# Attention with soft cap and a max-out layer: another order of weight loads, casts and filler matmuls at the start

## The chip, the cores and the metric

The kernel runs on one core of a Trainium2 chip. The metric is the device time of one execution in microseconds (us), as the median over several runs. The engines of the core are named PE (TensorE: matmuls and transposes), ACT (ScalarE: tanh, exp), DVE (VectorE), POOL (GpSimd) and SP (SyncE, which only issues transfers here). Transfers are issued by SP (a hardware queue) and by POOL (a software queue, which also converts float32 to bfloat16 on the way); both use the same 16 DMA engines.

## The reference

Attention over 8 batches and 12 heads, 448 positions, head dimension 64, and then a max-out layer on the 3584 tokens of 768 features:

```python
scores = scale * np.matmul(q, k.transpose(0, 1, 3, 2))
scores = cap * np.tanh(scores / cap)
attn = np.exp(scores - np.max(scores, axis=-1, keepdims=True))
attn = attn / (np.sum(attn, axis=-1, keepdims=True) + 1e-09)
x = np.matmul(attn, v)            # then (8, 12, 448, 64) -> (3584, 768)
g = np.maximum(x @ w1, x @ w2)    # w1, w2: 768 x 1024
out = g @ w_out                   # w_out: 1024 x 768
```

The inputs and the output are float32.

## The kernel before

**The algebra.** max(x w1, x w2) = x w2 + relu(x (w1 - w2)). So the kernel builds `wd_sb` = w1 - w2 and `wm_sb` = w2 w_out once, and computes out = x wm + relu(x wd) w_out. `wm_sb` costs PE work before the first output: `turn_w2(c)` transposes one of six chunks of w2 (8 matmuls against an identity, evicted by DVE into `w2T`), and `premultiply(c, half)` multiplies it with one half of w_out's columns (8 matmuls, evicted into `wm_sb`). Together that is 48 transposes and 96 matmuls.

**Tiles of the attention.** Two heads make a pair, 48 pairs in all; three pairs make a group g (16 groups), and two pairs a step t (24 steps, 0 to 23). `load` brings k, q or v of a group (or of one pair of it) through SP's queue, `cast` turns it to bfloat16 in `kqf` (k and q) or `vp` and `vl` (v). k and q must then be transposed into `qkT`: for pairs 0 to 5 (groups 0 and 1) PE does it with `transposes(i)`, 27 small matmuls and a DVE eviction; from group 2 on one DMA transpose by SP does a group, `cross(g)`. Then `scores(t, p)` makes the scores of one pair (p = 0, 1; three PSUM tiles j = 0, 1, 2) or the remaining keys of both (p = 2), each followed by a tanh on ACT; `ex(t, p)` takes the exponential of a whole p; `total(t)` sums it on PE and turns the sums into reciprocals on DVE (`st`, `rs`, `inv`); `values(t)` multiplies with v; `normalize(t)` writes `xT` on DVE. Step t uses pairs 2t and 2t + 1.

**Filler.** PE work that no step of the attention asks for stands in a list of generators, `fill_q`: first the w2 work, then `moe(b)` for each batch. `F(n)` takes n matmuls from it. Calls of `F` stand by hand between the calls of the attention, and each engine executes its instructions in the order in which they were written; so the numbers in `F` decide how much filler PE does ahead of the next scores. `moe(b)` has 8 groups of 6 matmuls (evicted by a relu on DVE) and for each tile of 128 rows two groups of 14 (evicted by a DVE copy to `osb`).

**Buffers that matter.** `mm_psum` has two tiles, shared by transposes, w2 work and MoE. `s_psum` has two and `v_psum` one; a score tile is free when its tanh is done. w2 itself lies in the tiles that later hold `gT` (the relu's output), so the relus wait until w2 has been used. w1 arrives in the tiles of later outputs (`osb`, and `xT` of batches 2 and 3), and `subtract` on POOL or DVE makes `wd_sb` of it.

**The order at the start.** On POOL's queue, transfers of w2 and w_out (`load_w2`, `load_wo`) alternate with casts: chunk 0, two pieces of w_out, chunk 1, the cast of pair 3, chunk 2, a piece of w_out, a one-element transfer (L517), the last piece of w_out, chunk 3, the casts of pair 4 and of half of v of group 0, chunk 4, the cast of pair 5, chunk 5. A cast waits for its load, and all that follows on POOL waits with it. The one-element transfer writes into the tile that pair 4's k is loaded into, so that SP's load of it (and all behind it on SP's queue) waits for that point of the software queue. Then come the calls of the attention for t = 0 to 3, with `F` between them, from L525 on, and a loop for t = 3 to 23 with 47 matmuls of filler in each pass.

Of the kernel before, what the change touches and what calls it, by code (L numbers as in the profile page):

```python
# [10 lines left out]
def kernel(  # L11
# [105 lines left out]
    def load(g, what, n0=0, n1=L):  # L117
        b, p = divmod(g * L, NP)
        h0, h1 = 2 * (p + n0), 2 * (p + n1)
        src = {"k": k, "q": q, "v": v}[what]  # L120
        t, m, l = raw_of(g, what)
        if g < NT:
            nc.sync.dma_start(
                out=t[:, n0 * S : n1 * S].rearrange("p (n c) -> p n c", c=S),
                in_=rows(src, b, h0, h1).rearrange("(n p) c -> p n c", p=P),
            )
            return
        nc.sync.dma_start(
            out=m[:, 2 * n0 : 2 * n1, :],
            in_=src[b, h0:h1, 0 : NJ * P, :].rearrange("h (p j) d -> p h (j d)", j=NJ),  # L130
        )
        if what == "q":
            nc.sync.dma_start(
                out=l[half(b), 2 * n0 : 2 * n1, :],
                in_=src[b, h0:h1, NJ * P : S, :].rearrange("h p d -> p h d"),
            )
        else:
            for par in range(2):
                nc.sync.dma_start(
                    out=l[64 * par : 64 * par + 64, n0:n1, :],  # L140
                    in_=src[b, h0 + par : h1 : 2, NJ * P : S, :].rearrange("h p d -> p h d"),
                )
# [65 lines left out]
    def load_wo(f, half):  # L208
        hs = slice(half * (DM // 2), (half + 1) * (DM // 2))
        nc.gpsimd.dma_start(  # L210
            out=wo_sb[:, f : f + FH, hs], in_=moe_w_out[f * P : (f + FH) * P, hs].rearrange("(c p) n -> p c n", p=P)
        )
# [5 lines left out]
    def load_w2(c):  # L218
        for part in range(2):
            nc.gpsimd.dma_start(out=w2b[part][:, c, :], in_=x_rows(moe_w2, c)[:, part * DH : (part + 1) * DH])  # L220
# [13 lines left out]
    w2T = {}  # L234

    def turn_w2(c):
        ps = mm_psum.tile([P, 512], f32, name="mm").bitcast(bf16)
        for f in range(FC):
            nc.tensor.transpose(ps[:, f * P : (f + 1) * P], w2b[f // FH][:, c, f % FH * P : (f % FH + 1) * P], ident)
            yield  # L240
        w2T[c] = stage.tile([P, FC * P], bf16, name="w2T", bufs=3)
        nc.vector.tensor_copy(w2T[c], ps)  # L242

    def premultiply(c, half):

        hs = slice(half * (DM // 2), (half + 1) * (DM // 2))
        ps = mm_psum.tile([P, 512], f32, name="mm")
        for f in range(FC):
            nc.tensor.matmul(  # L249
                ps[:, : DM // 2], w2T[c][:, f * P : (f + 1) * P], wo_sb[:, f, hs],  # L250
                start=(f == 0), stop=(f == FC - 1),
            )
            yield
        nc.vector.tensor_copy(wm_sb[:, c, hs], ps[:, : DM // 2])


# [139 lines left out]
    gT = {}  # L396

    def moe(b):
        if b % 2 == 0:
            gT[b // 2] = {}  # L400
        g, x = gT[b // 2], xT[b // 2]
        cs = slice((b % 2) * S, (b % 2 + 1) * S)
        for f in range(FC):
            ps = mm_psum.tile([P, 512], f32, name="mm")
            for c in range(KC):
                nc.tensor.matmul(  # L406
                    ps[:, :S], wd_sb[:, c, f * P : (f + 1) * P], x[:, c, cs], start=(c == 0), stop=(c == KC - 1)
                )
                yield
            if f // FH not in g:  # L410
                g[f // FH] = g_tile(f // FH)
            nc.vector.tensor_relu(g[f // FH][:, f % FH, cs], ps[:, :S])  # L412
        for t in range(3) if b % 2 == 0 else range(3, 7):
            osb = opool.tile([P, DF], f32, name="osb")[:, :DM]
            ts = slice(t * P, (t + 1) * P)
            for half in range(2):
                hs = slice(half * (DM // 2), (half + 1) * (DM // 2))
                ps = mm_psum.tile([P, 512], f32, name="mm")
                for c in range(KC):
                    nc.tensor.matmul(ps[:, : DM // 2], x[:, c, ts], wm_sb[:, c, hs], start=(c == 0), stop=False)  # L420
                    yield
                for f in range(FC):
                    nc.tensor.matmul(  # L423
                        ps[:, : DM // 2], g[f // FH][:, f % FH, ts], wo_sb[:, f, hs], start=False, stop=(f == FC - 1)
                    )
                    yield
                nc.vector.tensor_copy(osb[:, hs], ps[:, : DM // 2])  # L427
                if b == B - 1 and t == 6:
                    o = out[b * S : b * S + NJ * P, hs].rearrange("(p j) n -> p j n", j=NJ)
                    nc.sync.dma_start(out=o[:, NJ - 1, :], in_=osb[:, hs])  # L430
            if b == B - 1 and t == 6:
                continue
            wide = b * NP >= NT * L
            if t == 3:
                for n in range(2):
                    o = out[(b - 1 + n) * S : (b + n) * S, :]
                    to = o[NJ * P : S, :] if (b - 1 + n) * NP >= NT * L else o.rearrange("(r j) n -> r j n", j=R7)[:, R7 - 1, :]
                    nc.sync.dma_start(out=to, in_=osb[64 * n : 64 * n + 64, :])
            else:
                j = t if t < 3 else t - 4  # L440
                o = out[b * S : (b + 1) * S, :]
                if wide:
                    nc.sync.dma_start(out=o[: NJ * P, :].rearrange("(p j) n -> p j n", j=NJ)[:, j, :], in_=osb)
                else:
                    o = o.rearrange("(r j) n -> r j n", j=R7)
                    for n in range(2):
                        nc.sync.dma_start(out=o[:, 2 * j + n, :], in_=osb[64 * n : 64 * n + 64, :])

    fill_q = []
    rate = [1.0, 0.0]  # L450

    def F(n):
        rate[1] += n * rate[0]
        while rate[1] >= 1 and fill_q:
            try:
                next(fill_q[0])
                rate[1] -= 1
            except StopIteration:
                fill_q.pop(0)
        if not fill_q:  # L460
            rate[1] = 0.0
# [21 lines left out]
        for f, a in todo[i]:  # L483
            f(*a)

    def load_and_cast(g, n):
        for what in ("k", "q"):
            load(g, what, n, n + 1)
        for what in ("k", "q"):
            cast(nc.gpsimd, g, what, n, n + 1)  # L490

    for c in range(3):
        fill_q.append(turn_w2(c))
        fill_q.append(premultiply(c, 0))
    for c in range(3, KC):
        fill_q.append(premultiply(c - 3, 1))
        fill_q.append(turn_w2(c))
        if c > 3:
            fill_q.append(premultiply(c - 1, 0))
    fill_q.append(premultiply(KC - 3, 1))  # L500
    fill_q.append(premultiply(KC - 1, 0))
    for c in range(KC - 2, KC):
        fill_q.append(premultiply(c, 1))

    fill_const(nc.vector, 0)
    fill_const(nc.gpsimd, 1)
# [3 lines left out]
    load_w2(0)  # L510
    for f in range(0, FC, FH):
        load_wo(f, 0)
    load_w2(1)
    load_and_cast(1, 0)
    load_w2(2)
    load_wo(0, 1)
    nc.gpsimd.dma_start(out=raw_of(1, "k")[0][:1, S : S + 1], in_=moe_w_out[:1, :1])  # L517
    load_wo(FH, 1)
    load_w2(3)
    load_and_cast(1, 1)  # L520
    load(0, "v")
    cast(nc.gpsimd, 0, "v", halves=(1,))
    load_w2(4)
    load_and_cast(1, 2)
    load_w2(5)  # L525
    for n0, n1 in ((0, 1), (1, L)):
        for what in ("k", "q"):
            cast(nc.vector, 0, what, n0, n1)
# [2 lines left out]
    scores(0, 0, v_psum)  # L531
    ex(0, 0)
    transposes(1)
    F(8)
    scores(0, 1, v_psum)
    ex(0, 1)
    transposes(2)
    load(2, "k")
    load(2, "q")
    load(1, "v")  # L540
    cast(nc.gpsimd, 2, "k")
    cast(nc.gpsimd, 2, "q")
    cast(nc.gpsimd, 1, "v", halves=(1,))
    transposes(3)
    F(8)
    scores(0, 2)
    ex(0, 2)
    F(16)
    scores(1, 0, v_psum)
    ex(1, 0)  # L550
    F(16)
    scores(1, 1, v_psum)
    ex(1, 1)
    cast(nc.vector, 0, "v", halves=(0,))
    F(20)
    transposes(4)
    F(6)
    scores(1, 2)
    ex(1, 2)
    cross(2)  # L560
    for c in range(KC):
        load_w1(c, 0)
    load(3, "k")
    load(3, "q")
    for c in range(3):
        load_w1(c, 1)
    total(0)
    normalize(0, values(0))
    scores(2, 0, js=(0, 1))
    transposes(5)  # L570
    scores(2, 0, js=(2,))
    ex(2, 0)
    F(14)
    scores(2, 1, v_psum)
    F(6)
    cast(nc.vector, 1, "v", halves=(0,))
    F(8)
    scores(2, 2)
    ex(2, 1)
    total(1)  # L580
    normalize(1, values(1))
    F(4)

    scores(3, 0, v_psum)
    ex(2, 2)
# [6 lines left out]
        subtract(c, 1, nc.gpsimd)  # L592
    scores(3, 1, js=(0, 1))
    cross(3)
    for c in range(3, KC):
        load_w1(c, 1)
    load(2, "v")
    cast(nc.gpsimd, 2, "v")
    load(3, "v")
# [94 lines left out]
```

## Time and profile before

| | before |
|---|---|
| median of 13 runs | 354.59 us (352.87 to 356.83) |
| the profiled execution | 355.27 us |
| its span on the core | 353.3 us |
| PE busy | 329.1 us (93%) |
| ACT busy | 277.4 us (78%) |
| DVE busy | 229.8 us (65%) |
| POOL busy | 107.6 us (30%) |
| DMA, moved | 61.78 MB, mean 175 GB/s |

The span runs from the first to the last instruction of the core; all times inside the profile count from its start. Busy is the time in which an engine executes something; the difference to the span is idle time. A line of the page's slices has one digit for each of 40 equal slices of 8.8 us: the busy share in tenths. In a wait, the engine and line named first waited for what stands behind the arrow: total, how often, longest. In the chain of waits, each line is a start, a duration and what ran or was transferred.

### The profile page before, as it was taken

To read this page: it belongs to the slowest core of one execution; us is meant where nothing else is said; L and a number is where in the kernel's file an instruction comes from. 1 tells how busy PE (TensorE), PEld (TensorE's weight loads), DVE (VectorE), ACT (ScalarE), POOL (GpSimd) and SP (SyncE) were. 2 spreads that over 40 slices of the span, in tenths; PEclk is the share of its full clock that TensorE was granted. 3 is DMA by queue.
4 is the path that set the end of the run, shared out by engine and by line. 5 is a ranking of instruction groups with operands and counts; after the bars stand their busy time and mean duration, and the time that the engine had idled before them with its cause. 6 is when DMAs were issued, how large, how long until landed. Compare 5 with 4: busy or idle time off the path is not lost.

```text
span 353.3 us, 6833 instructions
## 1 busy us (share of the span) xinstructions
PE 329.1 (93%) x2722; PEld 164.9 (47%) x2722; DVE 229.8 (65%) x413; ACT 277.4 (78%) x241; POOL 107.6 (30%) x184
## 2 busy tenths in 40 slices
PE   3686797999999999999999999999999999999995
PEld 1343343445544554444544454445535554555563
DVE  5325387657768676877678667876777767883421
ACT  3948399989998999989998999999979998800000
POOL 6618367160341244124314431342144130000000
PEclk9999699999999999999999999999999999999999
DMA  7999897999798649973995599629973931012022
GB/s 220 195 263 270 160 300 167 258 248 225 119 254 253 126 130 232 312 158 102 236 297 111 136 234 315 145 78 215 303 171 94 198 105 45 2 46 89 0 91 89
DMA packets 106047, 61.78 MB, mean 175 GB/s; under 512 B 62624, under 2 KB 101024, under 8 KB 106016
## 3 DMA queue, kind: packets, MB, share of 16 engines
q1 hardware_dynamic: 102144, 58.21, 64.9%
q0 software_dynamic: 3872, 3.15, 5.9%
q8 instruction: 21, 0.34, 0.4%
q14 instruction: 10, 0.08, 0.1%
HBM read 42.47 MB, written 11.01 MB: 151 GB/s over the span
## 4 chain that ended last, share of the span: by engine, by line
PE 77%; DMA 8%; ACT 7%; DVE 4%; issue 1%; POOL 1%; SPq 1%; DVEq 0%; POOLq 0%
PE mm L423 21%; PE mm L406 19%; PE mm L420 16%; PE v L373 6%; PE s L310 5%; ACT tanh L311 4%; ACT expo L316 3%; PE s L307 2%; DMA gT<-in_moe_w_dram 2%; PE v L379 2%; PE v L310 2%; DMA qr<-in_q_dram 2%; DMA kr<-in_moe_w_out_dram 2%; DMA vr<-in_v_dram 2%; PE s L357 2%; DVE xT L394 1%
## 5 line engine op out<-in xcount | busy, mean ns | idle before, releaser
L316 ACT ACTIVATE expo<-tanh 128x2688 bf16<-128x2688 bf16 (+1 forms) x72 | 140.3, 1950 | 0.2
L311 ACT ACTIVATE tanh<-s 128x896 bf16<-128x896 f32 x122 | 106.5, 915 | 30.1 <-PE s L310 19.9
L423 PE MATMUL mm<-wo_sb,gT 128*128 128x384 bf16 x448 | 85.8, 327 | 0.0
L406 PE MATMUL mm<-xT,wd_sb 128*128 128x448 bf16 x384 | 78.7, 353 | 2.4 <-DVE gT L412 1.8
L420 PE MATMUL mm<-wm_sb,xT 128*128 128x384 bf16 x336 | 66.2, 327 | 0.0
L423 PEld LDWEIGHTS <-gT 128*128 128x128 bf16 x448 | 42.4, 98 | 34.4 <-issue 8.2
L427 DVE COPY osb<-mm 128x384 f32<-128x384 f32 x56 | 31.1, 556 | 41.4 <-PE mm L423 41.0
L406 PEld LDWEIGHTS <-wd_sb 128*128 128x128 bf16 x384 | 35.8, 98 | 40.5 <-issue 10.0
L412 DVE TENSOR_SCALAR gT<-mm 128x448 bf16<-128x448 f32 x64 | 39.4, 622 | 18.9 <-PE mm L406 18.4
L654 POOL COPY mark<-inv 1x1 f32<-1x1 f32 x18 | 3.2, 177 | 140.7 <-DVE inv L363 125.4
L420 PEld LDWEIGHTS <-xT 128*128 128x128 bf16 x336 | 31.6, 98 | 26.2 <-issue 6.3
L311 ACT ACTIVATE tanh<-v 128x896 bf16<-128x896 f32 x46 | 42.5, 925 | 0.0
L373 PE MATMUL v<-expo,vp 128*32 128x448 bf16 x576 | 36.8, 362 | 0.0
L359 DVE STREAM_TRANSPOSE st<-s 128x448 f32<-128x448 f32 x24 | 15.6, 650 | 27.3 <-PE s L357 17.4
L394 DVE TENSOR_TENSOR xT<-v,inv 128x448 bf16<-128x448 f32 x48 | 27.8, 620 | 4.0 <-PE v L379 1.7
L310 PE MATMUL s<-qkT 64*128 64x448 bf16 x196 | 28.2, 364 | 0.9 <-DVE qkT L281 0.8
L338 DVE TENSOR_TENSOR esum<-esum,expo 128x896 bf16<-128x896 bf16 x40 | 25.4, 634 | 1.0
L336 DVE TENSOR_TENSOR esum<-expo 128x896 bf16<-128x896 bf16 x40 | 25.6, 640 | 0.0
L334 DVE TENSOR_TENSOR esum<-esum,expo 64x896 bf16<-64x896 bf16 x40 | 24.6, 616 | 1.3
L310 PEld LDWEIGHTS <-qkT 64*128 64x128 bf16 x288 | 10.6, 95 | 24.4 <-issue 18.6
L249 PE MATMUL mm<-wo_sb,w2T 128*128 128x384 bf16 x96 | 19.2, 343 | 2.9 <-DVE w2T L242 2.9
L373 PEld LDWEIGHTS <-vp 128*32 128x32 bf16 x576 | 15.7, 99 | 11.0 <-issue 1.5
(66 smaller groups left out, 263.1 us busy)
## 6 DMA issues: line engine op xcount, KB each, us to landing
kr<-in_k_dram SPq DMA_DIRECT2D x14, 576.0 KB, 6.9
qr<-in_q_dram SPq DMA_DIRECT2D x14, 576.0 KB, 7.6
vr<-in_v_dram SPq DMA_DIRECT2D x14, 576.0 KB, 5.0
out_dram<-osb SPq DMA_DIRECT2D x20, 384.0 KB, 6.0
out_dram<-osb SPq DMA_DIRECT2D x16, 192.0 KB, 2.7
osb<-in_moe_w_dram SPq DMA_DIRECT2D x8, 256.0 KB, 4.5
gT<-in_moe_w_dram POOLq DMA_DIRECT2D x12, 128.0 KB, 7.2
wo_sb<-in_moe_w_out_dram POOLq DMA_DIRECT2D x4, 384.0 KB, 8.5
```

The costliest lines, as they stand in the source:

```text
L310: nc.tensor.matmul(s[:, m, :S], k0[r, j * P : (j + 1) * P], qTn[r, :])
L311: nc.scalar.activation(tanh[t, p][:, 2 * j : 2 * j + 2, :], s[:, :, :S], AF.Tanh, scale=scale / cap)
L316: nc.scalar.activation(expo[t, p], tanh[t, p][:, 0:n, :], AF.Exp, scale=float(cap))
L336: nc.vector.tensor_add(d, e_of(t, ab, 0), e_of(t, ab, 1))
L338: nc.vector.tensor_add(d, d, e_of(t, ab, 2))
L373: nc.tensor.matmul(ps[r, :S], vp[g % 2][:, 2 * n + h, j, u::2], e_of(t, ab, j)[:, h, :], start=(j == 0), stop=False,)
L394: nc.vector.tensor_mul(x_of(t, u), ps[:, u, :S], inv[t])
L406: nc.tensor.matmul(ps[:, :S], wd_sb[:, c, f * P : (f + 1) * P], x[:, c, cs], start=(c == 0), stop=(c == KC - 1))
L412: nc.vector.tensor_relu(g[f // FH][:, f % FH, cs], ps[:, :S])
L420: nc.tensor.matmul(ps[:, : DM // 2], x[:, c, ts], wm_sb[:, c, hs], start=(c == 0), stop=False)
L423: nc.tensor.matmul(ps[:, : DM // 2], g[f // FH][:, f % FH, ts], wo_sb[:, f, hs], start=False, stop=(f == FC - 1))
L427: nc.vector.tensor_copy(osb[:, hs], ps[:, : DM // 2])
```

## The change

On POOL's queue all of w2 and w_out is issued in one row, and the casts follow; the one-element transfer stands behind chunk 2. The cast of pair 3 moves to DVE. Transposes and scores of pairs 0 to 3 stand ahead of any w2 work. The w2 work has another order, in which a chunk is transposed one product ahead of its use, and the numbers in `F` follow it. `total(0)` and `normalize(0)` stand later than `values(0)`, and so on for step 1. On SP's queue two halves of w1 stand ahead of `cross(2)`, and all six second halves ahead of `cross(3)`. Last, the generators (`turn_w2` below, `premultiply` and `moe` in the same way) yield ahead of each matmul and not behind it, and `F` runs a generator to its end with its last matmul, so that a group's eviction is issued with its last matmul and not with the next call of `F`.

```diff
 def turn_w2(c):
-        ps = mm_psum.tile([P, 512], f32, name="mm").bitcast(bf16)
         for f in range(FC):
+            yield
+            if f == 0:
+                ps = mm_psum.tile([P, 512], f32, name="mm").bitcast(bf16)
             nc.tensor.transpose(ps[:, f * P : (f + 1) * P], w2b[f // FH][:, c, f % FH * P : (f % FH + 1) * P], ident)
-            yield
...
     def F(n):
         rate[1] += n * rate[0]
         while rate[1] >= 1 and fill_q:
+            g = fill_q[0]
+            if g is not rate[2]:
+                rate[2] = g
+                next(g)
+            rate[1] -= 1
             try:
-                next(fill_q[0])
-                rate[1] -= 1
+                next(g)
             except StopIteration:
                 fill_q.pop(0)
...
-    def load_and_cast(g, n):
+    def load_and_cast(g, n, eng=nc.gpsimd):
...
-    for c in range(3):
-        fill_q.append(turn_w2(c))
-        fill_q.append(premultiply(c, 0))
-    for c in range(3, KC):
-        fill_q.append(premultiply(c - 3, 1))
-        fill_q.append(turn_w2(c))
-        if c > 3:
-            fill_q.append(premultiply(c - 1, 0))
...
+    w2wo((0, T), (1, T), (0, 0), (2, T), (1, 0), (2, 0), (0, 1), (1, 1), (3, T), (2, 1), (3, 0), (4, T), (3, 1))
+    w2wo((4, 0), (5, T), (4, 1), (5, 0), (5, 1))
...
-    load_w2(1)
-    load_and_cast(1, 0)
-    load_w2(2)
-    load_wo(0, 1)
+    for c in range(1, 3):
+        load_w2(c)
     nc.gpsimd.dma_start(out=raw_of(1, "k")[0][:1, S : S + 1], in_=moe_w_out[:1, :1])
-    load_wo(FH, 1)
-    load_w2(3)
-    load_and_cast(1, 1)
-    load(0, "v")
-    cast(nc.gpsimd, 0, "v", halves=(1,))
-    load_w2(4)
-    load_and_cast(1, 2)
-    load_w2(5)
+    for f in range(0, FC, FH):
+        load_wo(f, 1)
+    for c in range(3, KC):
+        load_w2(c)
...
     transposes(1)
-    F(8)
     scores(0, 1, v_psum)
     ex(0, 1)
+    load_and_cast(1, 0, nc.vector)
     transposes(2)
+    transposes(3)
+    load_and_cast(1, 1)
+    load(0, "v")
+    cast(nc.gpsimd, 0, "v", halves=(1,))
+    load_and_cast(1, 2)
...
-    transposes(3)
-    F(8)
     scores(0, 2)
     ex(0, 2)
-    F(16)
+    F(28)
     scores(1, 0, v_psum)
     ex(1, 0)
-    F(16)
+    F(28)
     scores(1, 1, v_psum)
     ex(1, 1)
+    F(24)
+    transposes(4)
     cast(nc.vector, 0, "v", halves=(0,))
-    F(20)
-    transposes(4)
-    F(6)
     scores(1, 2)
     ex(1, 2)
+    for c in range(2):
+        load_w1(c, 0)
     cross(2)
-    for c in range(KC):
+    for c in range(2, KC):
         load_w1(c, 0)
     load(3, "k")
     load(3, "q")
-    for c in range(3):
+    for c in range(KC):
         load_w1(c, 1)
-    total(0)
-    normalize(0, values(0))
+    F(16)
     scores(2, 0, js=(0, 1))
-    transposes(5)
+    x0 = values(0)
     scores(2, 0, js=(2,))
     ex(2, 0)
-    F(14)
-    scores(2, 1, v_psum)
-    F(6)
+    transposes(5)
+    total(0)
+    F(8)
+    scores(2, 1, js=(0, 1))
+    normalize(0, x0)
+    F(4)
+    scores(2, 1, js=(2,))
     cast(nc.vector, 1, "v", halves=(0,))
-    F(8)
+    F(4)
     scores(2, 2)
     ex(2, 1)
+    F(8)
     total(1)
     normalize(1, values(1))
-    F(4)
+    F(2)
...
     cross(3)
-    for c in range(3, KC):
-        load_w1(c, 1)
```

More of the change, by code (lines that the diff above doesn't have):

```diff
@@ L246, in premultiply @@
         hs = slice(half * (DM // 2), (half + 1) * (DM // 2))
-        ps = mm_psum.tile([P, 512], f32, name="mm")
         for f in range(FC):
+            yield
+            if f == 0:
+                ps = mm_psum.tile([P, 512], f32, name="mm")
             nc.tensor.matmul(
@@ L252, in premultiply @@
             )
-            yield
         nc.vector.tensor_copy(wm_sb[:, c, hs], ps[:, : DM // 2])
@@ L398, in moe @@
     def moe(b):
-        if b % 2 == 0:
-            gT[b // 2] = {}
-        g, x = gT[b // 2], xT[b // 2]
+        g, x = gT.setdefault(b // 2, {}), xT[b // 2]
         cs = slice((b % 2) * S, (b % 2 + 1) * S)
         for f in range(FC):
-            ps = mm_psum.tile([P, 512], f32, name="mm")
             for c in range(KC):
+                yield
+                if c == 0:
+                    ps = mm_psum.tile([P, 512], f32, name="mm")
                 nc.tensor.matmul(
@@ L408, in moe @@
                 )
-                yield
             if f // FH not in g:
@@ L417, in moe @@
                 hs = slice(half * (DM // 2), (half + 1) * (DM // 2))
-                ps = mm_psum.tile([P, 512], f32, name="mm")
                 for c in range(KC):
+                    yield
+                    if c == 0:
+                        ps = mm_psum.tile([P, 512], f32, name="mm")
                     nc.tensor.matmul(ps[:, : DM // 2], x[:, c, ts], wm_sb[:, c, hs], start=(c == 0), stop=False)
+                for f in range(FC):
                     yield
-                for f in range(FC):
                     nc.tensor.matmul(
@@ L425, in moe @@
                     )
-                    yield
                 nc.vector.tensor_copy(osb[:, hs], ps[:, : DM // 2])
@@ L449 @@
     fill_q = []
-    rate = [1.0, 0.0]
+    rate = [1.0, 0.0, None]
     def F(n):
@@ L489, in load_and_cast, with w2wo @@
         for what in ("k", "q"):
-            cast(nc.gpsimd, g, what, n, n + 1)
-    for c in range(3):
-        fill_q.append(turn_w2(c))
-        fill_q.append(premultiply(c, 0))
-    for c in range(3, KC):
-        fill_q.append(premultiply(c - 3, 1))
-        fill_q.append(turn_w2(c))
-        if c > 3:
-            fill_q.append(premultiply(c - 1, 0))
[L500 to L503, printed above, removed]
+            cast(eng, g, what, n, n + 1)
+    def w2wo(*parts):
+        for c, half in parts:
+            fill_q.append(turn_w2(c) if half is None else premultiply(c, half))
+    T = None
+    w2wo((0, T), (1, T), (0, 0), (2, T), (1, 0), (2, 0), (0, 1), (1, 1), (3, T), (2, 1), (3, 0), (4, T), (3, 1))
+    w2wo((4, 0), (5, T), (4, 1), (5, 0), (5, 1))
     fill_const(nc.vector, 0)
```

## The prediction

> **What bounds the kernel now.** I read the page first: the totals, then the 40 slices.
>
> ```profile
> span 353.3 us, 6833 instructions
> PE 329.1 (93%) x2722; PEld 164.9 (47%) x2722; DVE 229.8 (65%) x413; ACT 277.4 (78%) x241; POOL 107.6 (30%) x184
> PE   3686797999999999999999999999999999999995
> ACT  3948399989998999989998999999979998800000
> ```
>
> From slice 8 on PE has no gap, so from about 66 us PE sets the pace; ACT is close behind (38.35 of 40 us in 110 to 150). What can be won lies in the first seven slices of 8.8 us. So I asked for stretches of 5 us (columns: stretch, then PE, PEld, DVE, ACT, POOL busy, PE clock, DMA share, GB/s).
>
> ```profile
> 25.00:30.00 5.00, 3.99 (x31) 1.97 (x29) 3.11 (x6) 4.97 (x5) 2.57 (x6) 1.00 1.08 307
> 30.00:35.00 5.00, 2.49 (x43) 1.51 (x40) 2.12 (x4) 4.23 (x4) 4.71 (x11) 1.00 1.13 247
> 35.00:40.00 5.00, 2.93 (x28) 1.12 (x32) 0.12 (x1) 1.72 (x2) 3.27 (x5) 0.61 0.63 113
> 40.00:45.00 5.00, 4.87 (x73) 2.31 (x66) 3.23 (x6) 1.95 (x4) 0.00 (x0) 0.71 1.06 244
> ```
>
> PE idles 7.9 us between 15 and 45, and from 36.1 to 42.9 it runs at half clock (0.50 in stretches of 1 us from 37 to 42): the 5.5 us of matmuls there would take half as long warm, 2.7 us less. Another 2.6 us idle lie in 45 to 60. These 13 us are all there is to take. The chain of waits, then the waits, say what the hole is:
>
> ```profile
> 20.76 6.75 DMA vr<-in_v_dram
> ...
> 29.40 7.63 DMA gT<-in_moe_w_dram
> ...
> 37.07 0.39 PE mm L239 x2
> 37.47 0.75 PE s L307 x2
> ```
>
> ```profile
> PE mm L239 <- DMA gT<-in_moe_w_dram: 4.5, 1, 4.5
> ACT tanh L311 <- PE s L307: 4.0, 1, 4.0
> ACT tanh L311 <- PE s L310: 3.0, 1, 3.0
> ```
>
> GpSimd stood behind v of group 0 until 27.5, cast it, and only at 29.40 issued w2 chunk 4. It landed at 37.0. PE stopped at its transpose with scores(1, 2) behind it; ACT dried up for 4.0 and then 3.0 us.
>
> **What the skill says.** "TensorE: Matmul & The Clock Gate", HAM clock gate: the array starts, and after an idle window of about 3.4 us falls back, at half clock, and about 3.4 us of work bring it back. The trace agrees: nothing between 32.6 and 37.07, half clock until 42.9; premultiplies take 0.34 us apart until 20, 0.18 from 22.5. "DMA: Bandwidth & Descriptors", Queues, rings and completion order: an engine takes turns between its queues packet by packet. The trace does not show that. By its packet records GpSimd's queue moved nothing until 7.0 (first issue 3.06), alone moved 192 to 207 KB per us from 10 to 21, and nothing from 23 to 33; at both borders one queue fades out while the other fades in. That looks like the order of issue, and I use it. The same page puts the fixed cost of a GpSimd transfer at about 2 us; here it hides behind a backlog.
>
> **The change, part by part.** *Transfers.* Bytes and count stay the same. GpSimd now issues all twelve w2 halves and four w_out pieces before any cast. At 200 KB/us a w2 chunk (256 KB as written) takes 1.3 us and a w_out piece (384 KB) 1.9. The one-element marker that holds back SP's pair 4 stands behind one w_out piece less: it lands at 19.9 - 1.9 = 18.0. GpSimd's later issues wait for landings eight transfers back, the last for the marker, so it is done at about 18.7 and no cast is held, since k of pair 4 lands later. In order of issue the second w_out half lands at 21.7, w2 chunks 3, 4, 5 at 23, 24.3, 26.7. SP's loads follow: k, q of pair 4 at 25 and 26, v at 28.8, group 2's q at 36.5 (35.0 before), v of group 1 at 38. Casting that q takes 1.14 + 0.51: cross(2) goes out at 38.3 (37.91 before).
>
> *Walk of PE and ACT*, with durations of the trace (tanh 0.92, large exp 2.44, small 0.96, evictions 0.56 to 0.69, a group of eight premultiplies 1.47 warm and 2.74 cold, eight w2 transposes 1.1 cold and 0.6 warm, values 2.26, total 1.1). VectorE casts pair 3 at 10.6 to 11.9 (GpSimd did it at 9.0 to 11.1; k and q landed at 9.0 and 10.5), so transposes 2 and 3 run 12.0 to 14.3 and scores(0, 2) at 14.3; its tanh waits only for exp(0, 1), to 17.0 instead of 20.95. The first 28 matmuls of w2 work fill 15.0 to 20.1: 1.2, a wait of 0.1 for chunk 1 (16.2), 1.1, 2.5, 0.3. Tanh(1, 0) starts at 20.5 (24.36 before). The next 28 (0.3 + 0.7 eviction overlapped, three groups of 1.47) end at 25.9, tanh(1, 1) at 26.3 (29.28). Then 24 (1.5, 0.6, 1.5), transposes 4 (0.85) and scores(1, 2), tanh 31.7 (38.25). Sixteen more, and scores(2, 0) at 34.0, tanh 34.4 (43.20). VectorE's half of the v cast (1.29 + 0.43 from 32.0) hides behind those 16; values(0) runs 34.6 to 36.9, transposes 5 to 38.1, total(0) to 39.2, a group to 40.7, tanh(2, 1) at 41.1 (48.12). Exp(2, 1) ends at 47.05, after scores(2, 2) at 43.0. VectorE then is the late one: v of group 1 cast from 42.6 to about 44.5 (1.93 + 1.14 beside GpSimd before), two evictions, total(1)'s statistics to 47.4; scores(3, 0) at 47.7, tanh 48.1 (53.80): 5.7 ahead. PE has no hole of 3.4 us, so it stays warm. cross(2) lands by 44.5.
>
> *From there ACT paces* (14.7 us busy of 15.6 between tanh(3, 0) and tanh(4, 1)); scores(4, 1), at 67.91 before, would stand at 62.2. But now all six second halves of w1 stand ahead of cross(3) on SP's queue, three more than before (0.79 MB, 2.6 us). From cross(2): four w1 halves to 47, group 3 to 52.5, six w1 halves to 57.5, cross(3) 4 us more: it lands at 62.5 (64.5 before). A stall of 0.3: the advance is 5.4.
>
> *Filler.* Up to scores(4, 1) the calls of F add to 166 now, 150 before: 16 more MoE matmuls of 0.194 us are behind us, 3.1. moe(0) has 132 matmuls; 6 + 47 + 47 + 38 = 138 are asked of it before moe(1) is appended at the end of t = 5, so six calls find nothing and their cover for the softmax adds is gone: at most 6 x 0.194 = 1.2 back, taken as 1.0.
>
> *Evictions with the last matmul.* The same instructions, earlier on VectorE's queue. What it can win is the PE waits for evictions after 66 us, 1.8 + 0.4 by the waits; what it can lose is a statistic of total queued behind an eviction of 0.56. VectorE is 74% busy there and the eviction follows a matmul that PE is just doing; I take 0, between -2 and +4.
>
> *Other moves at nothing:* two w1 halves ahead of cross(2) (1.6 us of transfers, behind v of group 1, which cross(2) waits behind anyway; without the 3 us between its landing and scores(3, 0) they would cost that), total(0) after values(0) (normalize is not asked for before scores(2, 1)).
>
> Sum: -5.4 - 3.1 + 1.0 = -7.5. The profiled execution took 355.27, of which 353.3 is the span; its span becomes 345.8. The median of the runs is 354.59, 0.7 below that execution, and it becomes 347.1; I say 347.0.
>
> **Rivals.** *cross(3) decides.* If packets are slower behind w1 (197 KB/us was seen at 31 us, with small pieces) and it lands at 66, the advance is 1.9 and the sum -1.9 - 3.1 + 1.0 = -4.0: 350.6. For it: DMA share above 1 from 45 to 55. Against: 2 us idle at 56 to 58 before.
>
> *Data come no sooner.* DMA is saturated from 4 to 36 in both and cross(2) is no earlier; if scores(3, 0) stays at 52.85, only the filler is won, 3.1 - 1.0: 352.5. Against: before, cross(2) landed at 43.5, nine us ahead of its use.
>
> *SP's queue goes first.* Then the second w_out half waits from 19.3 until SP's 4.2 MB are through, 36.5; PE, stopped at 25 for 11.5 us, also goes cold (1.7), and scores(2, 0) comes at 47.2 instead of 42.7, less 22 matmuls of filler (3.6): about 355.5. Against: 117 KB of GpSimd's queue still moved between 21 and 22 while SP's had begun.
>
> *Slower: evictions in front of the statistics.* If in each of 20 steady iterations one osb eviction of 0.56 stands ahead of the statistics of total, and PE waits for normalize, 11.2 us come back: 347.1 + 11.2 = 358.3. It decides from 0.37 us per iteration on (7.5 / 20). For it: 17.4 us of VectorE waiting for total, 19 times, so that chain is fresh when it starts. Against: the eviction ends inside total's own 1.1 us.
>
> **How the numbers follow.** My walk 0.60 (344 to 349.5), cross(3) 0.17, data no sooner 0.08, SP first 0.07, evictions 0.08. Left out of 344.0 to 352.6 are the last two and what exceeds the walk, under 0.2. About 0.3% is what a measurement of this kernel can tell from no change. Slower takes the evictions and a part of SP first, 0.10; the same, the rest of that and the weak end of data no sooner, 0.05; faster 0.85.
>
> **What would show it.** Right: no wait for gT above 1 us after 17; tanh(2, 0) near 34 and tanh(3, 0) near 48; no half clock between 25 and 60; GpSimd's queue busy to 25 without a break; cross(3) issued near 55 and PE waiting for it under 1 us; six fewer matmuls before the end of t = 5. Wrong: PE waiting for w_out near 25, PE waiting for a DMA transpose near 62, or more PE idle after 66 than the 2 to 3 us of before.

## The result and the profile after

| | before | changed |
|---|---|---|
| median | 354.95 us (48 runs, 352.34 to 358.12) | 344.6 us (11 runs, 343.55 to 347.01) |
| ratio | | 0.9717, 95% interval 0.9696 to 0.9739 |
| the profiled execution | 355.27 us | 343.37 us |
| its span | 353.3 us | 341.6 us |

The change makes the kernel 10.3 us faster, 2.8%. The forecast was 347.0, a gain of 7.5 on the 354.59 known then; the measured 344.6 lies near the lower end of its range, 344.0 to 352.6. The changed kernel's executions spread with the clock that PE was granted: the four of twelve with a mean of 0.998 or more took 343.4 to 344.2 us, the four at 0.990 or less 345.3 to 347.0, and the profiled one is the fastest.

The page of the changed kernel, totals and slices:

```profile
span 341.6 us, 6835 instructions
PE 324.7 (95%) x2722; PEld 163.8 (48%) x2722; DVE 230.6 (68%) x417; ACT 277.3 (81%) x241; POOL 107.9 (32%) x180
PE   3799989899999999999999999999999999999995
ACT  3979889789999999899989999999989999900000
```

Of the 11.7 us between the two spans, 4.4 are busy time of PE (329.1 to 324.7): the same 2722 matmuls, fewer of them at half clock (by the clock records, the clock is full from 22.4 us on before, with half clock again from 36.1 to 42.9; in the changed kernel it is full from 19.6 on). The other 7.3 are idle time (24.2 to 16.9). The stretches of 5 us, with the columns of before (stretch, then PE, PEld, DVE, ACT, POOL busy, PE clock, DMA share, GB/s), show where the hole was:

```profile
25.00:30.00 5.00, 4.80 (x59) 2.83 (x59) 2.27 (x4) 4.97 (x5) 1.88 (x4) 1.00 1.10 329
30.00:35.00 5.00, 5.00 (x83) 2.81 (x81) 3.08 (x6) 4.43 (x6) 3.56 (x8) 1.00 1.14 264
35.00:40.00 5.00, 4.44 (x42) 2.00 (x39) 4.44 (x9) 4.49 (x5) 3.39 (x5) 1.00 0.75 223
40.00:45.00 5.00, 4.54 (x67) 2.17 (x65) 4.09 (x9) 4.65 (x5) 0.69 (x1) 1.00 1.03 247
...
60.00:65.00 5.00, 3.73 (x23) 1.81 (x24) 2.30 (x5) 3.30 (x5) 0.06 (x1) 1.00 0.82 203
```

From 30 to 40 PE works 9.44 us instead of 5.42, and the clock column stays at 1.00. A new gap stands in 60 to 65. The waits between 15 and 66 us name it:

```profile
PE s L312 <- DMA qkT<-kqf: 2.2, 1, 2.2
PE mm L241 <- DMA gT<-in_moe_w_dram: 1.4, 2, 0.7
PE v L312 <- DVE xT L396: 1.0, 1, 1.0
```

The 4.5 us for chunk 4 of w2 are gone; what is left for w2 is 0.7 twice, chunk 1 at 15.8 and 17.1. In their place PE waits 2.2 us for cross(3). Other executions of the same program wait 1.8 to 3.8 us there (e8, e9, e12 below), which has consequences of its own. The chain of waits (start, duration, what) shows where that comes from: q of group 3 takes 8.43 us to land, POOL casts it, and the DMA transpose follows at once.

```profile
45.34 8.43 DMA qr<-in_q_dram
...
53.92 0.56 POOL kqf L181
...
55.13 0.52 POOL kqf L186
...
55.66 5.56 DMA qkT<-kqf
61.22 0.05 issue
61.27 0.55 PE s L312 x4
```

### The profile page after: what moved, and what is told of

It reads as the page before. It is cut to its first block, busy times and chain, and to the rows that moved or that the text cites. A ratio compares the mean times of both kernels' runs of the same rounds, so it can differ in the third digit from the quotient of the medians.

```text
span 341.6 us, 6835 instructions
## 1 busy us (share of the span) xinstructions
PE 324.7 (95%) x2722; PEld 163.8 (48%) x2722; DVE 230.6 (68%) x417; ACT 277.3 (81%) x241; POOL 107.9 (32%) x180
## 4 chain that ended last, share of the span: by engine, by line
PE 78%; DMA 10%; SPq 4%; DVE 4%; POOL 2%; issue 1%; POOLq 0%; DVEq 0%
PE mm L426 22%; PE mm L408 19%; PE mm L423 16%; PE v L375 6%; PE s L312 6%; DMA gT<-in_moe_w_dram 3%; DMA qr<-in_q_dram 2%; DMA vr<-in_v_dram 2%; PE v L312 2%; PE s L309 2%; PE v L381 2%; SPq L139 2%; PE s L359 2%; DMA qkT<-kqf 2%; SPq L133 1%
## 5 line engine op out<-in xcount | busy, mean ns | idle before, releaser
L313 ACT ACTIVATE tanh<-s 128x896 bf16<-128x896 f32 x123 | 107.4, 915 | 19.6 <-PE s L312 16.5
L429 DVE COPY osb<-mm 128x384 f32<-128x384 f32 x56 | 31.1, 555 | 44.8 <-PE mm L426 44.3
L426 PEld LDWEIGHTS <-gT 128*128 128x128 bf16 x448 | 42.3, 98 | 34.6 <-issue 8.5
L413 DVE TENSOR_SCALAR gT<-mm 128x448 bf16<-128x448 f32 x64 | 39.5, 622 | 20.5 <-PE mm L408 20.3
L313 ACT ACTIVATE tanh<-v 128x896 bf16<-128x896 f32 x45 | 41.6, 925 | 0.0
L375 PE MATMUL v<-expo,vp 128*32 128x448 bf16 x576 | 35.6, 353 | 0.0
L312 PE MATMUL s<-qkT 64*128 64x448 bf16 x198 | 28.3, 363 | 4.3 <-DMA qkT<-kqf 2.2
L338 DVE TENSOR_TENSOR esum<-expo 128x896 bf16<-128x896 bf16 x40 | 26.7, 669 | 0.0
L340 DVE TENSOR_TENSOR esum<-esum,expo 128x896 bf16<-128x896 bf16 x40 | 26.2, 656 | 0.8
L312 PEld LDWEIGHTS <-qkT 64*128 64x128 bf16 x288 | 10.4, 95 | 26.9 <-issue 16.7
L161 POOL CAST vp<-vr 128x1152 bf16<-128x1152 f32 x14 | 16.4, 1170 | 9.7 <-DMA vr<-in_v_dram 9.4
```

Of the source, the lines that this page charges most:

```text
L312: nc.tensor.matmul(s[:, m, :S], k0[r, j * P : (j + 1) * P], qTn[r, :])
L313: nc.scalar.activation(tanh[t, p][:, 2 * j : 2 * j + 2, :], s[:, :, :S], AF.Tanh, scale=scale / cap)
L338: nc.vector.tensor_add(d, e_of(t, ab, 0), e_of(t, ab, 1))
L340: nc.vector.tensor_add(d, d, e_of(t, ab, 2))
L375: nc.tensor.matmul(ps[r, :S], vp[g % 2][:, 2 * n + h, j, u::2], e_of(t, ab, j)[:, h, :], start=(j == 0), stop=False,)
L426: nc.tensor.matmul(ps[:, : DM // 2], g[f // FH][:, f % FH, ts], wo_sb[:, f, hs], start=False, stop=(f == FC - 1))
```

## The experiments

The first question was whether both parts of the change count, the second whether the row of transfers or the order of the calls does it. The others came out of the results.

### The evictions, alone and taken out (e1, e2)

e1 is the kernel before with the generators and `F` of the change; e2 is the changed kernel with those of before.

```diff
     def F(n):
...
+            g = fill_q[0]
+            if g is not rate[2]:
+                rate[2] = g
+                next(g)
```

> The kernel before with only the second part of the change (generators yield ahead of each matmul, evictions issued with a group's last matmul). The prediction took this part at 0 (-2 to +4). Theory: the PE waits for evictions after 66 us, 1.8 + 0.4 us before, are all that it can win, so -0.5 to -1.5 us, about 354. Rival: the part of the gain that the prediction missed (10.3 us measured against 7.5) comes from here: -2.5 us or more, 352 or below.

> The changed kernel with the generators and F of before (evictions issued with the next matmul of the filler). Theory: 0.5 to 1.5 us slower than the changed kernel, about 345.5, and the milestones up to 60 us stay (tanh(3, 0) near 44.5). Rival: 347 or above, because evictions of the w2 work come late in a stretch where only two PSUM tiles are there for transposes, w2 work and MoE.

e1 measured 354.12 us, ratio 0.9987 (0.9969 to 1.0005); e2 measured 346.79, ratio 0.9746 (0.9701 to 0.9791). e1's interval holds "no effect" and "1 us" and excludes its rival. e2's reaches, against the changed kernel, from no effect to 2.6 us, so it excludes neither the 0.5 to 1.5 us of the theory nor the rival (347 or above). The stretch from 80 to 335 us, first of before, then of the changed kernel, gives the size:

```profile
80.00:335.00 255.00, 253.01 (x2019) 125.66 (x2017) 184.63 (x327) 217.67 (x190) 65.04 (x108) 1.00 0.66 163
```

```profile
80.00:335.00 255.00, 253.98 (x2013) 127.08 (x2006) 180.29 (x320) 210.13 (x183) 64.86 (x108) 1.00 0.65 163
```

PE idles 1.99 us in 255 before and 1.02 after; in e1 it is 1.66, in e2 1.69. So at most 1 us is here. e2's rival is about the time ahead of 80 us. There e2's trace lies among those of the changed kernel: tanh(3, 0) starts at 44.4 and tanh(5, 0) at 73.5, against 44.5 and 71.1 in the profile above and 43.7 and 73.2 in that of e9, which is the changed kernel again. No loss of the rival's size shows.

With the calls of before it is otherwise. In e1 the first eviction into `w2T` starts at 12.2 us instead of 16.7, and tanh(1, 0) at 21.0 instead of 24.4. Then PE waits 3.5 us for an eviction that stands behind VectorE's cast of v, and 5.3 us for chunk 4, and tanh(2, 0) starts at 43.2 in both kernels. So the old hole swallows 3.4 us that the evictions win, and e1 does not say what they would be worth without it. In the new calls they are not resolved beyond "about 1 us".

### The row of transfers, alone and taken out (e3, e4)

```diff
-    load_w2(1)
-    load_and_cast(1, 0)
-    load_w2(2)
...
+    for c in range(1, 3):
+        load_w2(c)
...
+    for c in range(3, KC):
+        load_w2(c)
```

e3 puts this into the kernel before, e4 takes it out of the changed one. The places of the casts go with it: pair 3 on DVE and the others behind the row, or all of them between the transfers.

> The kernel before with only POOL's transfers in one row ahead of its casts (and the cast of pair 3 on DVE, since POOL would come to it late); calls, F and SP's w1 loads as before. Theory: PE's wait for chunk 4 (4.5 us) and the half clock that follows (2.7 us) go, but the filler of before is used up in the same places, so ACT gains what the hole cost it: about 5 us, 349 to 350. Rival, the calls alone do it: the row is worth under 1.5 us, 353 or more.

> The changed kernel with POOL's queue of before (casts between the transfers, cast of pair 3 on POOL). Theory: chunk 4 is asked for at 31.5 us and is issued only behind the cast of v of group 0, near 29.5, so it lands near 36: PE stands 4 to 5 us, goes to half clock, and about 5 us of the gain are lost: 349 to 351. Rival, the calls alone do it: 346 or less.

e4 measured 351.24 us, ratio 0.9885 (0.9835 to 0.9936): in the new calls the row is worth 6.6 us, a little more than the 5 expected. Its wait for chunk 4 is back, and so is the half clock, from 34.6 to 44.8 us by the clock records:

```profile
PE mm L241 <- DMA gT<-in_moe_w_dram: 5.9, 2, 5.1
```

```profile
35.00:40.00 5.00, 1.53 (x12) 0.82 (x12) 0.41 (x2) 0.00 (x0) 3.16 (x5) 0.50 1.33 214
```

(The first line is from e4's waits between 28 and 46, the second from its stretches.)

e3 measured 356.58 us, ratio 1.0033 (1.0009 to 1.0058). With the calls of before the row is worth nothing; it even costs. That is the number of the rival (353 or more), but not its reason: e4 shows that the calls alone do not do it. The trace says why. These are lines of the timeline (start, duration, engine, line, what, idle before and its releaser), first of the kernel before, then of e3:

```profile
58.17 0.75 PE L350 MATMUL s<-expo,ones 128*32 128x448 bf16 x12 [1.47 <-ACT tanh L311]
```

```profile
52.16 0.75 PE L350 MATMUL s<-expo,ones 128*32 128x448 bf16 x12 [1.47 <-ACT tanh L311]
...
69.76 4.46 PE L406 MATMUL mm<-xT,wd_sb 128*128 128x448 bf16 x12 [4.99 <-DVE gT L412]
```

total(2) starts at 52.16, where it started at 58.17 before: the row did win 6 us. Then PE stands 4.99 us for a relu on VectorE, and the matmuls behind it run at half clock (12 in 4.46 us). VectorE's side of it, from e3's waits between 52 and 74:

```profile
PE mm L406 <- DVE gT L412: 5.0, 1, 5.0
...
DVE wd_sb L232 <- DMA osb<-in_moe_w_dram: 2.9, 1, 2.9
DVE wd_sb L232 <- DMA xT<-in_moe_w_dram: 2.8, 1, 2.8
```

VectorE stood at the subtractions for chunks 3 to 5 of `wd_sb`, whose second halves of w1 come behind cross(3) in this kernel. The relus stand behind them in VectorE's queue; without a relu no `mm` tile comes free, and PE stops. The attention was 6 us early, w1 was not: the last of these halves landed at 68.4 in e3 and at 67.0 before.

### The place of w1 (e5, e6)

So the next question was the six halves of w1 ahead of cross(3), which the prediction had counted as a cost. e5 adds their new place to e3, e6 takes it out of the changed kernel.

```diff
-    for c in range(3):
+    for c in range(KC):
         load_w1(c, 1)
...
     cross(3)
-    for c in range(3, KC):
-        load_w1(c, 1)
     load(2, "v")
```

> The kernel of e3 (POOL's transfers in one row, calls of before) with the second w1 halves 3 to 5 moved ahead of cross(3), as in the changed kernel. Theory: in e3 the row advanced the attention by 6 us (total(2) at 52.2 instead of 58.2), and then VectorE stood at the subtractions of exactly these halves, so that the relus behind them came late and PE stood 5.0 us; with the halves ahead of cross(3) this wait goes, and the row's 5 to 6 us show: 349 to 351. cross(3) then lands later, and PE waits for it 1 to 2 us more. Rival: PE would have stood at cross(3) anyway, so nothing is won: 355 to 357.

> The changed kernel with the second w1 halves 3 to 5 behind cross(3), as before. The prediction counted their place ahead of cross(3) as a cost (2.6 us of transfers). Theory now: PE's wait of 2.2 us for cross(3) shrinks, but the halves land near 65 us, VectorE stands at their subtraction, PE behind it for 3 to 5 us and perhaps at half clock after it: 347 to 351. Rival, the prediction's reading: 1 to 2 us faster than the changed kernel, 343.

e5 measured 351.37 us, ratio 0.9912 (0.9883 to 0.9941), 5.2 us below e3: the wait for VectorE is gone from this stretch, one for cross(3) of 2.5 us stands there, with half clock behind it from 64.4 to 67.8. That is just above the 349 to 351 expected. e6 measured 349.46 us, ratio 0.9841 (0.9789 to 0.9893), 4.9 us above the changed kernel. The waits of e6 between 52 and 72:

```profile
DVE wd_sb L232 <- DMA osb<-in_moe_w_dram: 5.2, 1, 5.2
...
PE mm L408 <- DVE wd_sb L232: 3.5, 3, 2.1
...
PE s L312 <- DMA qkT<-kqf: 3.0, 1, 3.0
```

The halves come late and PE waits 3.5 us for them, and its clock is at 0.70 from 65 to 70. The wait for cross(3) did not shrink (3.0 us), against the expectation too: cross(3) was issued at 55.72 and landed at 61.19, in the changed kernel at 55.66 and 61.22. It was not held by w1. Both rivals fall.

Put together, in medians:

| transfers of POOL | second halves of w1 | calls | us |
|---|---|---|---|
| as before | as before | as before | 354.95 |
| in one row | as before | as before | 356.58 |
| in one row | ahead of cross(3) | as before | 351.37 |
| in one row | as before | new | 349.46 |
| as before | ahead of cross(3) | new | 351.24 |
| in one row | ahead of cross(3) | new | 344.6 |

The last three rows also have the new evictions and the two first halves of w1 ahead of cross(2); "calls" stands for all of that. Each of the three parts is worth 5 to 7 us when the other two are in place (6.8 for the calls, from 351.37 to 344.6). Against a later series of the changed kernel (345.78, e9 below) each is 1.2 us less. The row on a kernel with the old calls and the old place of w1 is worth less than nothing. They are links of one chain, not gains that add.

### How a transfer of POOL starts (e8, e12)

```diff
+            if t in (6, 18):
+                nc.gpsimd.dma_start(out=probe, in_=x_rows(moe_w2, 0)[:, : DF // 2])
```

> The changed kernel with two more transfers on POOL's queue (one half chunk of w2 into a tile that nobody reads) at the end of steps 6 and 18, behind the mark. It asks why POOL's first transfer moved nothing for 4 us (issued 3.06, first packet 7.0; issued 29.4, first packet 33.0) while SP's queue was busy. If a POOL transfer takes some 4 us to start in any case, the packets come 3.5 to 4 us after the issue also in step 18, where the DMA engines are nearly idle. If it waited for SP's queue to drain, they come within 1 to 2 us in step 18.

> As e8, with the extra POOL transfer at the end of steps 3, 4, 5, 7 and 8. In e8 the packets came 1.3 and 1.2 us after the issue, with SP's queue empty. At the end of step 3 SP's queue is full (250 to 290 KB per us until 76). If POOL's transfer waits for SP's queue to drain, its packets there come 4 us or more after the issue, and without interleaving; if the engines take turns, they come within 2 us and one by one between SP's.

By the packet records, with SP's queue running empty the first packet came 1.3 and 1.2 us after the issue (e8; the times of these kernels, 346.03 and 343.93, are of one run each). In e12, step 3, with SP's queue moving 190 to 313 KB per us:

```profile
69.44 0.58 POOL L658 DMA_DIRECT2D probe<-in_moe_w_dram  x1
```

```profile
probe<-in_moe_w_dram POOLq DMA_DIRECT2D x1, 128.0 KB, 7.0
```

The issue, and the time to landing, 7.0 us. Its first packet came at 73.5, 4.1 us after the issue, and from then to 76.0 its 144 packets lay among SP's, which went on (338, 447 and 412 packets of SP in 73, 74 and 75). Steps 4, 5, 7 and 8 gave 2.2, 2.5, 1.2 and 2.5 us; at step 7, the one of 1.2, SP's queue was running empty. So neither reading is the whole: with SP's queue in use a POOL transfer starts up to 3 us later than with SP's queue empty, but it does not wait for SP's queue to drain. Why it starts later is not shown.

### More of w1 ahead of cross(2) (e7, e9, e10, e11)

The DMA engines run dry while SP waits for POOL's cast of group 2. In the changed kernel, columns as above:

```profile
37.00:38.00 1.00, 1.00 (x9) 0.31 (x7) 0.97 (x3) 1.00 (x1) 0.53 (x2) 1.00 0.49 176
38.00:39.00 1.00, 0.73 (x4) 0.30 (x4) 1.00 (x3) 1.00 (x2) 0.91 (x2) 1.00 0.11 34
```

```diff
-    for c in range(2):
+    for c in range(4):
         load_w1(c, 0)
     cross(2)
-    for c in range(2, KC):
+    for c in range(4, KC):
         load_w1(c, 0)
```

> The changed kernel with four first halves of w1 ahead of cross(2) instead of two. The DMA engines run dry there (156 KB at 37 us, 34 KB at 38) while SP waits for POOL's casts of group 2. Theory: 0.52 MB, 1.6 us of transfers, move into that hole, all that SP issues behind cross(2) lands up to 1.6 us sooner, and PE's wait for cross(3) falls from 2.2 to about 0.7: 343.2. Rival: ACT paces that stretch and takes the time back, or cross(2) is delayed: 344.6 or more.

> The changed kernel itself, for comparison on one chip with the next two: near 344.6.

> The kernel of e7 again, beside the changed kernel: in e7 the wait for cross(3) fell from 2.2 to 0.3 us, and a new one of 2.5 us for cross(2) came. Theory: ACT, which paces the stretch from 45 to 61, is ahead by less than the two waits say, 0.5 to 2.5 us faster than e9. Rival: no difference beyond 1 us, and e7 was another chip's 342.

> The changed kernel with three first halves of w1 ahead of cross(2). Theory: half of both effects, the wait for cross(2) under 1.5 us and the wait for cross(3) near 1.3; within 1 us of e10. Rival: the wait for cross(2) costs nothing, since ACT is the later one there; then it lies between e9 and e10.

e7 measured 342.4 us, ratio 0.9647 (0.9607 to 0.9688). In a later series on one chip, the changed kernel (e9) gave 345.78 us, ratio 0.9732 (0.9697 to 0.9767), four first halves (e10) 342.61, ratio 0.9652 (0.9620 to 0.9683), and three (e11) 343.85, ratio 0.9693 (0.9660 to 0.9726). e9 lies 1.2 us above the 344.6 of the first series. The intervals of e9 and e10 don't meet: about 3 us, more than the 0.5 to 2.5 expected, and a version that beats both kernels. PE's waits for the DMA transposes between 15 and 66, first of e9, then of e10:

```profile
PE s L312 <- DMA qkT<-kqf: 4.8, 2, 3.4
```

```profile
PE s L312 <- DMA qkT<-kqf: 1.4, 1, 1.4
```

The two waits of e9 are 4.8 us, of which e10 keeps 1.4, the one for cross(2): 3.4 less. That the medians differ by 3.2 is not simply this sum, as the stretch from 60 to 65 shows, first of e9, then of e10:

```profile
60.00:65.00 5.00, 3.33 (x14) 1.33 (x15) 1.70 (x3) 2.87 (x4) 0.00 (x0) 0.76 0.85 192
```

```profile
60.00:65.00 5.00, 5.00 (x29) 2.26 (x28) 3.85 (x7) 4.97 (x6) 1.60 (x3) 1.00 0.92 259
```

In e10, q of group 3 lands at 52.2 instead of 54.2 and cross(3) at 60.1 instead of 61.6, so tanh(4, 1) starts 1.2 us sooner than in e9. But e9's wait of 3.4 us is also followed by half clock from 62.6 to 66.0, and at tanh(4, 2) the lead of e10 is 2.9 us. Against the first profile of the changed kernel, which has no half clock there, e10's last tanh comes only 0.8 us sooner (293.5, 294.3).

The wait for cross(2), 2.5 us in e7 and 1.4 in e9 and e10, does delay ACT (tanh(3, 0) starts at 45.6 in e7, 43.7 in e9). It does not cost its length, because scores(4, 1) stands for cross(3) in e9 in any case. e11 lies between, too close to either side to be told apart.

Four traces have the program of the changed kernel up to cross(3), since the extra transfers of e8 and e12 come later:

| | PE's wait for cross(3) | half clock behind it | tanh(3, 0) | tanh(5, 0) |
|---|---|---|---|---|
| e12 | 1.8 us | none | 44.8 | 71.1 |
| first profile | 2.2 us | none | 44.5 | 71.1 |
| e9 | 3.4 us | 3.4 us | 43.7 | 73.2 |
| e8 | 3.8 us | 3.4 us | 43.9 | 73.8 |

The two that were ahead at tanh(3, 0) are behind at tanh(5, 0). cross(3) lands at 61.2 to 62.2 in all four, so who comes earlier waits longer, and behind the two longer waits the clock was at half.

## Why the prediction was right, and where its sizes were off

**The hole and its cause: right.** PE's wait for chunk 4 and the half clock behind it are gone with the row, and back without it (e4). The clock gate of the Trainium skill ("TensorE: Matmul & The Clock Gate", HAM clock gate) agrees with e3 and e4: their waits of 5.0 and 5.1 us are followed by 6.8 and 10.2 us of half clock. The length of a wait alone does not decide it: 2.5 us in e5 are followed by half clock, 2.5 us in e7 are not (the last section has more). That PE stays warm, as the prediction says, held in the first profile, but not in e8 and e9.

**The walk: right in order, too slow.** Predicted and measured starts of the tanh are, in us: scores(0, 2) 17.0 and 16.7; (1, 0) 20.5 and 20.6; (1, 1) 26.3 and 25.5; (1, 2) 31.7 and 30.4; (2, 0) 34.4 and 32.5; (2, 1) 41.1 and 38.4; (3, 0) 48.1 and 44.5. The step that failed is the durations; five of the six stretches between these starts are 0.5 to 0.9 us shorter than predicted. A row of eight premultiplies in the timeline is 1.47 us long, but that includes the drain of the last one, which the next matmul overlaps. Put one after the other they are shorter, as this line of the changed kernel shows:

```profile
21.05 4.06 PE L252 MATMUL mm<-wo_sb,w2T 128*128 128x384 bf16 x24
```

Three groups take 4.06 us, not 4.41. In the same way values(0) took 1.69 us (32.53 to 34.22), not 2.26, and total(0) 0.94, not 1.1. The trace of before already had these sizes: values(1) runs there from 50.68 to 52.38, 1.70 us, and 2.26 is the sum of its four rows, which overlap. VectorE's cast of v for group 1, which was to make VectorE the late one, took 1.54 us (39.17 to 40.71) and not nearly 2. Differences of this kind add up to the 3.6 us at tanh(3, 0); not every one was measured alone. (Two details of the change bear on this walk: ahead of any w2 work stand the transposes of pairs 0 to 3, but of the scores only those of pairs 0 and 1, and the scores of pairs 2 and 3 follow behind 28 and 56 of its matmuls; and total(1) still stands ahead of values(1).)

**cross(3): the mechanism was seen, the size was off.** It landed at 61.2 (62.5 predicted), but scores(4, 1) was ready for it at 59.1, not 62.2, so PE waited 2.2 us and not 0.3. (The prediction's own steps, 57.5 and 4 us more, give 61.5 and not 62.5: a slip of 1.0.) The advance there is 67.91 - 61.27 = 6.6 instead of 5.4. That it came out so near is in part luck: PE was 3.1 us earlier than walked, and the landing of cross(3) took most of that back. What the prediction had wrong is why cross(3) is late. It put it down to the six halves of w1 ahead of it, at 2.6 us; e6 moved three of them away, and the wait stayed. cross(3) goes out when POOL has cast q of group 3, whose larger part lands at 53.8; where fewer halves of w1 stand between cross(2) and this load, as in e10, q lands 1.9 us and cross(3) 1.6 us sooner than in e9.

**The place of w1 as a cost: wrong in sign.** The prediction put no price on the halves coming late. e6, and e3 against e5, say what it is: about 5 us.

**Filler.** The 16 matmuls are there: 22 MoE matmuls stand ahead of scores(4, 1), 6 before, worth 3.1 us. That six calls of `F` find nothing at the end of t = 5 was taken as 1.0 us; PE's only wait there is 0.18 us, for `xT`. This term should have been 0.2.

**Order of issue: wrong.** The prediction took the engines to serve the two queues in the order of issue. In the changed kernel both have work from 22 to 28 us, and at first they move equal numbers of packets. Packets by us, from the packet records:

```
us      POOL's queue   SP's queue
21      180            44
22      114            111
23      106            108
24      113            114
25      103            105
```

That fits what the Trainium skill says ("DMA: Bandwidth & Descriptors", Queues, rings and completion order: each engine takes turns between its queues, packet by packet), and I had read the trace against it. What had misled me was probably the late start that e12 measured. For SP's loads it did not matter here: k of pair 4 landed at 23.4 (25 predicted), v of group 0 at 28.3 (28.8), group 2's q at 36.4 (36.5). The w2 chunks 3, 4 and 5 paid for it, at 24.1, 26.8 and 29.4 instead of 23, 24.3 and 26.7, but PE asked for them later still.

**The sum.** In spans: 6.6 (advance) + 3.1 (filler) - 0.2 (the empty `F`) = 9.5, and 1.0 less idle time after 80, of 11.7. The remaining 1.2 us lie between scores(4, 1) and 80 us and are not attributed. In medians the gain is 10.3; the two profiled executions lie 0.3 above and 1.2 below their medians, which makes the rest.

**The rivals.** *cross(3) decides* came true in part, at 2.2 us and while PE was further ahead than it assumed; PE waiting for a DMA transpose near 62 was on the prediction's list of signs of being wrong. *Data come no sooner* fell: cross(2) went out at 37.62, 0.3 us earlier than before, it had slack as said, and scores(3, 0) came at 43.99 instead of 52.85. *SP's queue first* fell with the packets above. *Evictions in front of the statistics* fell with e1, which is not slower than the kernel before.

## What to carry to other kernels

When a start-up is limited by one wait, look up what stands right behind it before pricing the fix: here the row of transfers was worth 6.6 us or nothing, depending on whether the next operand (w1) and the next filler were in time. A transfer placed early has a price of its bytes, and a transfer placed late has the price of every instruction queued behind its consumer; only the first is visible in the profile of a kernel that does not yet wait for it. In a walk along a queue, take start-to-start distances from the trace, not the lengths of merged rows. And before pricing a wait from one trace, look at a second execution: here the same program waited 1.8 to 3.8 us at the same place.

## What the hardware showed that was not expected

A transfer issued on POOL's queue moved its first packet 1.2 to 1.3 us after the issue when SP's queue was running empty (both cases of e8, one of e12), and 2.2 to 4.1 us after it in the four cases of e12 with SP's queue in use. The other way round, SP's first packet behind POOL's backlog came 1.2 us after its issue in the kernel before (19.91, 21.15) and 3.6 us in the changed one (18.02, 21.58). When both queues of the changed kernel then had work, they moved equal numbers of packets (114 and 111, 106 and 108, 113 and 114 in successive us). Alone, POOL's converting transfers write 192 to 207 KB per us.

The changes of PE's clock lie on a grid. Within each kept trace they stand 3.41 us or a whole multiple of it apart, and the place of the grid differs from one execution to the next. Counted over the 14 kept traces (some 1400 cells of 3.41 us, busy time by the matmul records), the clock went to half only behind cells in which PE was busy 0 to 53% of the time, and stayed full only behind cells of 42% and more; it went back to full behind cells of 81% and more. So it matters where in the grid a wait falls: e5's wait of 2.5 us lies inside one cell (61.0 to 64.4, 26% busy) and is followed by half clock, e7's wait of 2.5 us is divided by a border at 44.1 and is not. The first profile's wait of 2.2 us is divided in the same way at 60.6, and its cells stay at 56% and more; that this execution has no half clock there is partly the luck of its grid.
